# Dividing the probabilities of late heads by their sums, and a second q and k set for odd early heads, in a planned fp32r attention and MLP kernel

## The chip, the cores and the metric

The kernel runs on one core of a Trainium2 chip. The metric is device time in microseconds (us), the median of three runs. Engines are called as in the profile: PE (TensorE matmuls), PEld (its weight loads), DVE (VectorE), ACT (ScalarE), POOL (GpSimd), SP (the queue that issues all DMAs).

## What is computed

Three stages follow one another on 4 batches of 8 heads, 576 positions and 64 values a head, all in fp32:

```python
scores = q @ k.T / 8 + (cum[i] - cum[j])    # cum: running sum of log(clip(f)); causal mask
attn = exp(scores - max); attn /= sum(attn) + 1e-9
x = attn @ v                                # heads side by side: 2304 tokens x 512
x = ((x @ w1) * (x @ w2)) @ w3 @ w_out      # 512 -> 1024 -> 1024 -> 512
x = x / rms(x) * g
out = (silu(x @ w_gate) * (x @ w_val)) @ moe2_w_out   # 512 -> 1536 -> 512
```

## The kernel before

**Number format.** Every fp32 operand of a matmul is split into a high and a low part of the type fp32r, and a product takes two or three matmuls. So each matrix that TensorE reads costs two more passes of another engine: a copy that gives the high part, and a difference that gives the low part.

**A head.** `prep` makes Q1 (high part of q/8 on partitions 0 to 63, low part on 64 to 127), Q2, K1 and K2 from the loaded q and k: Q1's high part (line 348) and K1 (line 349) on ACT, Q2 (line 238, through `scaled`) and K2 (line 230, through `sub`) on an engine that the planner picks, Q1's low part on DVE (line 352). Four more rows of Q2 and K2 carry cum, so that the matmuls of `attn_s` (lines 367 and 368) give scores with their decay. There is one set of Q1, Q2, K1, K2 for all heads: `prep` of a head can't write it before the matmuls of the head before have read it. `row_max` (DVE, line 384) adds the mask and takes the row maximum, `row_exp` (ACT, line 391) takes exp and the row sums. `attn_t` transposes the probabilities on PE (line 428) and splits them into PTh (ACT, line 431) and PTl (DVE, line 432). `pv` multiplies by v (lines 451 and 457) and adds two halves into x.

**The pair.** Two heads share a 128-row block of x. Once a pair is through, the inverse sums (lines 413 and 414) are spread by a copy into rcol (640 columns, through `scaled`), five matmuls transpose rcol (line 473, `normalize`), and DVE multiplies x by it from PSUM (line 477).

**The weights.** Twenty raw units of 1 MB (w3, w_out, then w1 with w2) are loaded as bit patterns and rebuilt by `unit`: ACT (line 496), DVE (lines 497 and 498), then the high part on ACT (line 504) and the low part by `sub`. `wc_group` forms w3 @ w_out on PE (line 557), evicted by lines 560 and 561. The first MLP is `ab_group` (line 590) and `y_group` (line 613), the second one line 714 and line 745.

**The order.** All operations go into a `Plan`. `begins` walks back from the end and gives each operation a latest begin; for PE operations the due time `at` can make it earlier. `order` simulates the engines with assumed durations and emits a static program order for each engine. An operation with several engines is only taken by one on which, in the simulation, it ends first:

```python
end = min(begin(i, x, k) + m for x, m, k in ops[i][0])
if t + ns > end + 1:
    continue
```

For such a copy of n columns the assumed durations are 95 + 0.833 n ns on ACT, 70 + 0.52 n on DVE, 170 + 0.83 n on POOL. Operations marked `lock` on DVE and all on POOL exclude each other in the simulation. Among those ready, an engine takes the one with the smallest latest begin plus `WAIT` times its wait. The due times come from constants: heads of the first batch every `TE`, later ones every `T1`, the groups of w3 @ w_out every `WCP` from `WC0`. The first MLP of batch 0 is due `FD` after the last head of batch 0, and heads of batch 1 are mixed with it.

Of the kernel before, what the change touches and what calls it, by code (L numbers as in the profile page):

```python
# [69 lines left out]
class Plan:  # L70
# [54 lines left out]
    def order(self):  # L125
# [10 lines left out]
        dma = 0  # L136
# [59 lines left out]
def body(ctx, tc, q, k, v, f, w12, w3, wo1, wgv, wo2, g, out):  # L196
# [9 lines left out]
    def pe(cols, fn, r=(), w=(), at=0, times=1):  # L206

        plan.op([("PE", times * (max(110, 0.4475 * cols) + 2), False)], lambda e: fn(), r, w, at)
# [81 lines left out]
    Wch = [m1.tile([P, DM], F32R, name=f"Wch{i}") for i in range(KF)]  # L290
    Wcl = [m1.tile([P, DM], F32R, name=f"Wcl{i}") for i in range(KF)]
# [38 lines left out]
    def make_qk_rows():  # L330
        for t in (Q2, K2):
            V.memset(f32(t)[D:P, :], 0.0)
# [12 lines left out]
    def prep(h, at):  # L345
        p = h % 2
        a, b_ = rq[p][0:D], rk[p]
        act(S, lambda: A.activation(Q1[0:D, :], a, AF.Copy, scale=0.125), [("rq", p)], ["Q1h"], at)
        act(S, lambda: A.copy(K1, b_), [("rk", p, 0), ("rk", p, 1)], ["K1"], at)
        scaled(S, Q2[0:D, :], a, 0.125, [("rq", p)], ["Q2"])  # L350
        low = dict(out=Q1[D:P, :], in0=a, scalar=0.125, in1=f32(Q1[0:D, :]), op0=ALU.mult, op1=ALU.subtract)
        dve(S + 100, lambda: V.scalar_tensor_tensor(**low), [("rq", p), "Q1h"], ["Q1l"], at, lock=True)
        sub(S, K2[0:D, :], b_[0:D], f32(K1[0:D, :]), [("rk", p, 0), "K1"], ["K2"])
        if h:
            dma(9200, lambda: SP.dma_start(out=f32(Q2[D:D + 4, :]), in_=cq_d[h]), ["cdq"], ["rowq"], at)
            dma(9200, lambda: SP.dma_start(out=f32(K2[D:D + 4, :]), in_=cn_d[h]), ["cdn"], ["rown"], at)

    QK = ["Q1h", "Q1l", "Q2", "K1", "K2", "rows", "rowq", "rown"]

    def prep_v(h, at):  # L360
        p = h % 2
        scaled(5 * D, V2[p][:, :, 0:D], rv[p], 1.0, [("rv", p)], [("V2h", p)])
        sub(5 * D, V2[p][:, :, D:P], rv[p], f32(V2[p][:, :, 0:D]), [("rv", p), ("V2h", p)], [("V2", p)])

    def s_main(o, i, k0, k1):
        q0, n = QB[i]
        T.matmul(o, Q1[:, q0:q0 + n], K1[:, k0:k1], start=True, stop=False)  # L367
        T.matmul(o, Q2[:, q0:q0 + n], K2[:, k0:k1], start=False, stop=True)  # L368

# [7 lines left out]
    def row_max(h, ap, i, key, at):  # L377
# [4 lines left out]
        if len(ap.shape) == 3:  # L382
            o, m = (x.rearrange("p (c n) -> p c n", c=2) for x in (o, m))
        dve(cols + 12, lambda: V.tensor_tensor_reduce(out=o, in0=ap, in1=m, scale=-1.0, scalar=-NEG, op0=ALU.add, op1=ALU.min, accum_out=nmax[p][:n, i:i + 1]),  # L384
            ["mask"], [("nmax", p, i), ("PB", p, i), key], at)

    def row_exp(h, i, at):
# [3 lines left out]
        act(cols + 110, lambda: A.activation(o, o, AF.Exp, bias=nmax[p][:n, i:i + 1], scale=-1.0, accum_out=rsum[pr][:n, p, i:i + 1]),  # L391
            [("nmax", p, i)], [("PB", p, i), ("rsum", pr, p, i)], at)

    def attn_s(h, at):
        p = h % 2
        t = wide.rearrange("p (c n) -> p c n", c=2)
# [45 lines left out]
    def pv(h, at):  # L442
        p, j, (b, pp) = h % 2, h % 2, divmod(h // 2, H // 2)
        t = wide
# [14 lines left out]
        pe(192, tail, [(a, c) for a in ("PTh", "PTl") for c in (PT_KB0, PT_KB3)] + [("V2", p), ("V2h", p)], ["wide"], at, 2)  # L459
        x_to, x_key = X[b % 2][j * D:(j + 1) * D, pp, :], ["wide", ("x", b % 2, pp, j)] + [("raw", "x1")] * (b == 1)  # L460
        act(S, lambda: A.copy(half, t[D:P, 0:S]), [], ["half", "wide"], at, 55)
        dve(S + 100, lambda: V.tensor_add(x_to, t[0:D, 0:S], half), ["half"], x_key, at)

    def normalize(h, at):
# [3 lines left out]
        t = wide  # L468
# [7 lines left out]
        pe(128, run, ["rcol"], ["wide"], at, 5)  # L476
        dve(S, lambda: V.tensor_mul(x, x, t[:, 0:S]), [], ["wide"] + [("x", b % 2, pp, j) for j in range(2)], at)
# [3 lines left out]
    def unit(raw, key, src, h_l, outkey, at, at_load, r_load=(), w_load=(), r_out=(), over=None, parts=1):  # L481
# [14 lines left out]
        act(1024, lambda: A.activation(f32(hi()), f32(hi()), AF.Prelu, scale=2.0**-112, alpha=2.0**32), [key], [kh], at)  # L496
# [3 lines left out]
        for c in range(parts):  # L500
# [48 lines left out]
    def wc_group(i, at, step):  # L549
# [10 lines left out]
        act(512, lambda: A.copy(Wch[i], o), [], [("bank", n), ("Wch", i)], at)  # L560
        dve(512, lambda: V.tensor_sub(Wcl[i], o, f32(Wch[i])), [("Wch", i)], [("bank", n), ("Wcl", i)], at)
# [3 lines left out]
    speed = [FR]  # L565
# [15 lines left out]
    def ab_group(b, c, fb, m):  # L581
# [23 lines left out]
    def y_group(b, c, eb):  # L605
# [160 lines left out]
    def attention(h):  # L766
        if h < NH:
            attn_s(h, s_at(h))
        if h:
# [3 lines left out]
            if h % 2 == 0:  # L773
# [8 lines left out]
    def start():  # L782
# [6 lines left out]
        dve(1150, make_qk_rows, w=["rows", "Q2", "K2"], at=-100)  # L789
# [4 lines left out]
        dve(300, lambda: V.tensor_copy(hi.bitcast(F32R), cum), ["cum"], ["cq0"], -100)  # L794
        dve(S, lambda: V.tensor_sub(lo.bitcast(F32R), cum, hi), ["cum", "cq0", "cq1"], ["cq"], -100)
# [25 lines left out]
    start()  # L821
    units = [("w3", 0)] + [("wo", i) for i in range(4)] + [("w3", i) for i in range(1, KF)] + [("w12", i) for i in range(KF)]
    where = ["nrm", "ul", "x", "x1"][:NRAW]
    for n, (kind, i) in enumerate(units):
# [3 lines left out]
        raw = where[n % NRAW] if n < 16 else "nrm" if i % 2 else "w3"  # L828
        {"w3": w3_unit, "wo": wo_unit, "w12": w12_unit}[kind](i, raw, 0, 0)
# [106 lines left out]
```

## Time and profile before

| | before |
|---|---|
| median of 3 runs | 1038.04 us (1037.55 to 1038.85) |
| profiled execution | 1038.35 us, its span 1036.6 us |
| PE busy | 992.6 us, 96% of the span |
| DVE busy | 555.5 us, 54% |
| ACT busy | 466.1 us, 45% |
| POOL busy | 186.8 us, 18% |

The time is that of the program with what lies around its span, here 1.75 us more than the span. A share of the whole span is a mean over stages: heads and weights come first, the second MLP fills the last 450 us.

### The profile page before, as it was taken

To read this page: it belongs to the slowest core of one execution; us is meant where nothing else is said; L and a number is where in the kernel's file an instruction comes from. 1 tells how busy PE (TensorE), PEld (TensorE's weight loads), DVE (VectorE), ACT (ScalarE), POOL (GpSimd) and SP (SyncE) were. 2 spreads that over 40 slices of the span, in tenths; PEclk is the share of its full clock that TensorE was granted. 3 is DMA by queue.
4 is the path that set the end of the run, shared out by engine and by line. 5 is a ranking of instruction groups with operands and counts; after the bars stand their busy time and mean duration, and the time that the engine had idled before them with its cause. 6 is when DMAs were issued, how large, how long until landed. Compare 5 with 4: busy or idle time off the path is not lost.

```text
span 1036.6 us, 15402 instructions
## 1 busy us (share of the span) xinstructions
PE 992.6 (96%) x5928; PEld 886.8 (86%) x5928; DVE 555.5 (54%) x1104; ACT 466.1 (45%) x1004; POOL 186.8 (18%) x222
## 2 busy tenths in 40 slices
PE   1799979999999999999999999999999999999997
PEld 1578869999999999999999888878888888888896
DVE  6889999757668676776557445532122112211121
ACT  4778887656665665665445434421121112111111
POOL 3535433322523132240220300000000000000000
PEclk9999989999999999999999999999999999999999
DMA  8554533111212121200432324312001000100000
GB/s 271 184 189 134 181 116 120 49 36 51 71 37 61 48 60 39 59 15 1 170 120 105 136 109 162 104 59 84 1 1 41 1 1 0 41 1 1 17 25 21
DMA packets 28161, 75.71 MB, mean 73 GB/s; under 512 B 3644, under 2 KB 12348, under 8 KB 23160
## 3 DMA queue, kind: packets, MB, share of 16 engines
q1 hardware_dynamic: 28088, 74.73, 22.1%
q8 instruction: 46, 0.75, 0.3%
q14 instruction: 27, 0.22, 0.1%
HBM read 64.69 MB, written 10.03 MB: 72 GB/s over the span
## 4 chain that ended last, share of the span: by engine, by line
PE 91%; DVE 6%; DMA 1%; ACT 1%; issue 1%; POOL 0%; ACTq 0%; DVEq 0%; POOLq 0%
PE bank L714 29%; PE bank L590 19%; PE bank L613 10%; PE wide L745 8%; PE bank L745 6%; PE bank L428 5%; PE wide L451 4%; PE bank L557 3%; PE bank L368 1%; PE bank L367 1%; PE wide L473 1%; PE wide L367 1%; PE wide L368 1%; PE wide L457 1%; DMA rk<-in_k 1%
## 5 line engine op out<-in xcount | busy, mean ns | idle before, releaser
L721 DVE TENSOR_TENSOR s<-bank,s 128x512 f32<-128x512 f32 (+1 forms) x60 | 38.3, 638 | 281.3 <-PE bank L714 281.3
L714 PE MATMUL bank<-xnh,wgh 128*128 128x512 f32 (+1 forms) x480 | 177.6, 370 | 0.0
L714 PE MATMUL bank<-xnl,wgh 128*128 128x512 f32 (+1 forms) x480 | 177.6, 370 | 0.0
L714 PE MATMUL bank<-xnh,wgl 128*128 128x512 f32 (+1 forms) x480 | 177.2, 369 | 0.0
L720 ACT ACTIVATE s<-bank 128x512 f32<-128x512 f32 (+1 forms) x60 | 33.3, 555 | 189.4 <-PE bank L714 189.2
L714 PEld LDWEIGHTS bank<-xnh,wgh 128*128 128x128 f32 x480 | 90.2, 188 | 16.9
L714 PEld LDWEIGHTS bank<-xnl,wgh 128*128 128x128 f32 x480 | 90.3, 188 | 16.4
L714 PEld LDWEIGHTS bank<-xnh,wgl 128*128 128x128 f32 x480 | 90.2, 188 | 16.1
L431 ACT CAST PTh<-bank 128x320 fp32r<-128x320 f32 (+3 forms) x128 | 64.7, 506 | 86.5 <-PE bank L428 74.4
L722 ACT CAST zh<-s 128x512 fp32r<-128x512 f32 (+1 forms) x60 | 34.7, 578 | 129.7 <-DVE s L721 129.7
L432 DVE TENSOR_TENSOR PTl<-bank,PTh 128x320 fp32r<-128x320 f32 (+3 forms) x128 | 74.7, 588 | 22.2 <-ACT PTh L431 21.4
L613 PE MATMUL bank<-uh,Wch 128*128 128x288 f32 x256 | 77.2, 302 | 0.0
L613 PE MATMUL bank<-ul,Wch 128*128 128x288 f32 x256 | 75.5, 295 | 0.0
L613 PE MATMUL bank<-uh,Wcl 128*128 128x288 f32 x256 | 75.3, 294 | 0.0
L723 DVE TENSOR_TENSOR zl<-s,zh 128x512 fp32r<-128x512 f32 (+1 forms) x60 | 39.1, 652 | 30.4 <-ACT zh L722 30.0
L451 PE MATMUL wide<-PTh,V 128*128 128x512 f32 (+4 forms) x160 | 53.2, 338 | 0.6 <-DVE nmaxb L384 0.5
L451 PE MATMUL wide<-PTl,V 128*128 128x512 f32 (+4 forms) x160 | 49.6, 326 | 1.9 <-DVE PTl L432 1.9
L596 ACT COPY a<-bank 128x288 f32<-128x288 f32 x64 | 25.6, 400 | 52.7 <-PE bank L590 52.4
L745 PE MATMUL wide<-wo2h,zh 128*128 128x512 f32 x120 | 47.9, 399 | 0.7 <-ACT o L755 0.7
L613 PEld LDWEIGHTS bank<-uh,Wch 128*128 128x128 f32 x256 | 48.1, 188 | 0.4
L613 PEld LDWEIGHTS bank<-ul,Wch 128*128 128x128 f32 x256 | 48.2, 188 | 0.3
L598 DVE TENSOR_TENSOR u<-bank,a 128x288 f32<-128x288 f32 x64 | 29.1, 455 | 35.5 <-PE bank L590 30.5
(281 smaller groups left out, 2589.2 us busy)
## 6 DMA issues: line engine op xcount, KB each, us to landing
raw<-in_wgv SPq DMA_DIRECT2D x12, 1024.0 KB
rk<-in_k SPq DMA_DIRECT2D x64, 144.0 KB
raw<-in_wo SPq DMA_DIRECT2D x6, 1024.0 KB
nrm<-in_w SPq DMA_DIRECT2D x5, 1024.0 KB
rv<-in_v SPq DMA_DIRECT2D x32, 160.0 KB
rq<-in_q SPq DMA_DIRECT2D x32, 144.0 KB
yn_d<-nrm SPq DMA_DIRECT2D x8, 576.0 KB
raw<-yn_d SPq DMA_DIRECT2D x4, 1024.0 KB
```

The source lines that it names most:

```text
L428: T.transpose(o[:, c * P:(c + 1) * P], PB[p][i][:, kb * P:(kb + 1) * P], ident)
L431: act(n, lambda: A.copy(PTh[:, pt:pt + n], o[:, lo:lo + n]), [], [("PTh", pt), key], at, 55)
L432: dve(n, lambda: V.tensor_sub(PTl[:, pt:pt + n], o[:, lo:lo + n], f32(PTh[:, pt:pt + n])), [("PTh", pt)], [("PTl", pt), key], at)
L451: pe(w, lambda s_=s_, o=o, w=w, c=c, kb=kb, m=m, src=src: T.matmul(t[:, o:o + w], V2[p][:, kb, :], src[:, c:c + w], start=(s_ == 0 and m = ...
L590: T.matmul(o, a, x[:, kt, :], start=(kt == 0 and i == 0), stop=(kt == KD - 1 and i == 2))
L613: T.matmul(o, a[:, es], x[:, ft, :], start=(ft == 0 and i == 0), stop=(ft == KF - 1 and i == 2))
L714: T.matmul(t[m], a[:, m, kt, :], x[:, kt, 0:n], start=(kt == 0 and i == 0), stop=(kt == KD - 1 and i == 2))
L720: act(n, lambda: A.activation(s_()[:, 0:n], t[0], AF.Silu), [("bank", b_[0]), "right"], ["s"], at)
L721: dve(n, lambda: V.tensor_mul(s_()[:, 0:n], t[1], s_()[:, 0:n]), [("bank", b_[1])], ["s"], at)
L722: act(n, lambda: A.copy(zh()[:, 0:n], s_()[:, 0:n]), ["s"], [("zh", zp)], at)
L723: dve(n, lambda: V.tensor_sub(zl()[:, 0:n], s_()[:, 0:n], f32(zh()[:, 0:n])), ["s", ("zh", zp)], [("zl", zp)], at, lock=True)
L745: T.matmul(acc2[t], a[:, ts_], w, start=(fb == 0 and i == 0), stop=(fb == KF2 - 1 and i == 2))
```

## The change

For heads from 8 on (`LATE`), the sums are inverted head by head, and the five probability blocks of the head (64, 192, 320, 448 and 576 columns) are multiplied by them in place, by copies with a free engine, before they are transposed. These pairs have no rcol, no transposes of it and no product on x. Heads 0 to 7 keep the old way.

In batch 0, odd heads get a q and k set of their own (`qk2`, in space that the first MLP uses later as `uh`). Its zero rows are set by DVE or POOL. The factor 1/8 leaves `prep` and goes into `row_max`; cum is scaled by 8 to fit. Q1's high part, K1 and the high parts of rebuilt weights become copies with a free engine, and Q1's low part a difference on DVE or POOL. At the start, the high part of cum goes to ACT, and the negated rows to a free engine.

The planner's constants change, several assumed durations become longer (the scores of 512 columns to 680 and 570, exp by 115 columns), and a rule is added: before it takes an operation that begins later, an engine takes one that fits ahead of it, with `SLIP` of overrun. After `MT` the simulated hand-over between engines is longer by 600 and 300 ns and not by 321 and 133.

```diff
+LATE = 8
-S0, TE, T1 = 14000, 11400, 14300
-LT, LP = 8000, 10500
-WC0, WCP = 30000, 9400
-FD, FR = 14000, 1.48
-WAIT = 2.0
-COLD = 19378
-MT, MARGIN, MARGIN2 = 135119, 321, 133
+S0, TE, T1 = 0, 9000, 14300
+LT, LP = 5000, 13000
+WC0, WCP = 20000, 9400
+FD, FR = 14000, 1.35
+WAIT, SLIP = 2.0, 800
+DMA0, COLD = 4500, 26000
+MT, MARGIN, MARGIN2 = 135000, 600, 300
...
+                fits = [c for c in can if c[0] < t and c[0] + c[2] < t + SLIP]
+                if fits:
+                    t, i, ns, lock = min(fits, key=lambda c: (by[c[1]] + WAIT * (c[0] - first), c[1]))
...
+    qk2 = get("qk2", m1, [P, 4, S], F32R, tag="uh", name="qk2")
+    def qk_of(h):
+        i = h % 2 if h < H else 0
...
-        act(S, lambda: A.activation(Q1[0:D, :], a, AF.Copy, scale=0.125), [("rq", p)], ["Q1h"], at)
-        act(S, lambda: A.copy(K1, b_), [("rk", p, 0), ("rk", p, 1)], ["K1"], at)
-        dve(S + 100, lambda: V.scalar_tensor_tensor(**low), [("rq", p), "Q1h"], ["Q1l"], at, lock=True)
+        copy(S, lambda: Q1()[0:D, :], a, [("rq", p), ("rows", s_)], [("Q1h", s_)])
+        copy(S, K1, b_, [("rk", p, 0), ("rk", p, 1), ("rows", s_)], [("K1", s_)])
+        sub(S, lambda: Q1()[D:P, :], a, lambda: f32(Q1()[0:D, :]), [("rq", p), ("Q1h", s_)], [("Q1l", s_)])
...
+        if h >= LATE:
+            sums, inv = rsum[pr][:, p], rinv[pr][:, p]
+            dve(10, lambda: V.tensor_scalar_add(inv, sums, 1.0e-9), ...)
+            dve(80, lambda: V.reciprocal(inv, inv), [], [("rinv", pr, p)], at)
+            for i in (1, 2, 3, 4, 0):
+                n, cols = QB[i][1], QEND[i]
+                o = PB[p][i][:n, 0:cols]
+                copy(cols, o, o, [("rinv", pr, p)], [("PB", p, i)], rinv[pr][:n, p, i:i + 1])
...
-            act(n, lambda cs=cs: A.copy(h_l()[0][:, cs], f32(lo()[:, cs])), [key, kl] + r_out, wh, at)
+            copy(n, lambda cs=cs: h_l()[0][:, cs], lambda cs=cs: f32(lo()[:, cs]), [key, kl] + r_out, wh)
...
-            if h % 2 == 0:
+            if h % 2 == 0 and h <= LATE:
                 normalize(h - 1, at + LP)
...
-        dve(300, lambda: V.tensor_copy(hi.bitcast(F32R), cum), ["cum"], ["cq0"], -100)
+        act(S, lambda: A.activation(hi.bitcast(F32R), cum, AF.Copy, scale=8.0), ["cum"], ["cq0"], -100)
-        dve(S, lambda: V.tensor_scalar_mul(cn[:, 1::2, :], cq[:, 0::2, :], -1.0), ["cq", "cn1"], ["cn"], -90)
+        copy(2 * S, cn[:, 1::2, :], cq[:, 0::2, :], ["cq", "cn1"], ["cn"], -1.0)
```

## Rows read from the trace of the kernel before

**Rows 1.** The profile page: span and busy time of each engine.
```profile
span 1036.6 us, 15402 instructions
...
PE 992.6 (96%) x5928; PEld 886.8 (86%) x5928; DVE 555.5 (54%) x1104; ACT 466.1 (45%) x1004; POOL 186.8 (18%) x222
```

**Rows 2.** Stretches: length, then PE, PEld, DVE, ACT, POOL busy, clock, DMA.
```profile
15.00:60.00 45.00, 30.17 (x134) 24.02 (x135) 38.83 (x72) 33.37 (x67) 16.78 (x16) 0.92 0.69 225
60.00:130.00 70.00, 69.08 (x399) 58.65 (x398) 62.25 (x133) 58.03 (x140) 32.35 (x37) 1.00 0.48 157
130.00:155.00 25.00, 18.02 (x109) 15.52 (x110) 24.45 (x47) 20.12 (x38) 7.58 (x7) 0.86 0.35 117
155.00:200.00 45.00, 44.28 (x331) 42.73 (x330) 38.69 (x76) 31.42 (x72) 16.05 (x15) 1.00 0.29 89
200.00:500.00 300.00, 300.00 (x2276) 294.26 (x2275) 207.08 (x501) 177.74 (x458) 82.71 (x99) 1.00 0.17 48
```

**Rows 3.** Timeline of PE: start, us, what; idle before and its releaser.
```profile
14.92 0.58 PE L367 MATMUL wide<-K,Q 128*128 128x288 f32 x1 [14.92 <-DVE Q L352]
...
16.49 0.58 PE L368 MATMUL wide<-K,Q 128*128 128x288 f32 x1 [0.99 <-DVE K L810]
...
143.16 0.82 PE L590 MATMUL bank<-xhl,W0h 128*128 128x288 f32 x2 [4.35 <-DVE Wcl L561]
```

**Rows 4.** Line 473, transposes of rcol: ns min/median/max, first and last start.
```profile
L473 PE MATMUL wide<-ident,rcol x80: 270/272/328, 53.7 to 491.7; 128*128 128x128 f32 x80
```

**Rows 5.** Timeline of PE around the last such group: start, us, what.
```profile
491.24 0.71 PE L473 MATMUL wide<-ident,rcol 128*128 128x128 f32 x5
491.70 0.38 PE L613 MATMUL bank<-uh,Wch 128*128 128x288 f32 x1
491.92 0.29 PE L613 MATMUL bank<-ul,Wch 128*128 128x288 f32 x1
492.05 0.29 PE L613 MATMUL bank<-uh,Wcl 128*128 128x288 f32 x1
```

**Rows 6.** DVE's groups up to 150 us: busy us, mean ns, idle before.
```profile
L352 DVE SCALAR_TENSOR_TENSOR Q<-rq,Q 64x576 fp32r<-64x576 f32 x11 | 8.5, 772 | 1.5 <-ACT Q L348 1.1
...
L498 DVE SCALAR_TENSOR_TENSOR x<-x 128x1024 uint32<-128x1024 uint32 x4 | 6.2, 1560 | 0.0
...
L498 DVE SCALAR_TENSOR_TENSOR raw_x<-raw_x 128x1024 uint32<-128x1024 uint32 x4 | 4.9, 1222 | 0.1
...
L497 DVE TENSOR_SCALAR raw_x<-raw_x 128x1024 uint32<-128x1024 uint32 x4 | 4.1, 1029 | 0.0
...
L497 DVE TENSOR_SCALAR nrm<-nrm 128x1024 uint32<-128x1024 uint32 x4 | 2.7, 687 | 0.0
...
L794 DVE CAST x<-tmp 68x576 fp32r<-68x576 f32 x1 | 1.6, 1608 | 0.0
...
L813 DVE TENSOR_SCALAR x<-x 32x1152 f32<-32x1152 f32 x1 | 0.7, 747 | 0.0
```

**Rows 7.** The longest wait of DVE from 15 to 150 us.
```profile
DVE PTl L432 <- ACT PTh L431: 6.0, 15, 0.8
```

**Rows 8.** Line 238, copies of which the planner picks the engine: ns min/median/max.
```profile
L238 POOL TENSOR_SCALAR Q<-rq x32: 663/667/677, 7.3 to 454.2; 64x576 fp32r<-64x576 f32 x32
L238 POOL TENSOR_SCALAR V<-rv x27: 447/458/1397, 13.2 to 460.6; 128x320 fp32r<-128x320 f32 x27
L238 DVE TENSOR_SCALAR rcol<-rinvb x6: 819/820/821, 78.1 to 476.6; 128x640 f32<-128x640 f32 x6
L238 DVE TENSOR_SCALAR rcol<-rinva x4: 820/820/822, 52.7 to 451.4; 128x640 f32<-128x640 f32 x4
```

**Rows 9.** Line 230, the differences K2 that went to POOL.
```profile
L230 POOL TENSOR_TENSOR K<-rk,K x22: 1388/1422/2454, 9.5 to 459.2; 64x576 fp32r<-64x576 f32 x22
```

**Rows 10.** ACT's copies of q and k up to 150 us.
```profile
L348 ACT ACTIVATE Q<-rq 64x576 fp32r<-64x576 f32 x11 | 7.5, 684 | 1.3 <-issue 1.2
L349 ACT CAST K<-rk 128x576 fp32r<-128x576 f32 x11 | 7.4, 671 | 0.1
```

More of the change, by code (lines that the diff above doesn't have):

```diff
@@ L206, in pe @@
     def pe(cols, fn, r=(), w=(), at=0, times=1):
[L208 removed]
+        plan.op([("PE", times * (max(110, 0.4475 * cols) + 2), False)], lambda e, times=times: fn(), r, w, at)
     def t_dve(n, rate=1.04, lock=False):
@@ L328, in make_zeros, with get, fn, make_qk_rows @@
             G.memset(t, 1.0)
-    def make_qk_rows():
+    lazy = {}
+    def get(key, pool_, shape, dtype, **kw):
+        def fn():
+            if key not in lazy:
+                lazy[key] = pool_().tile(shape, dtype, **kw) if callable(pool_) else pool_.tile(shape, dtype, **kw)
+            return lazy[key]
+        return fn
+    Wch = get("Wch", m1, [P, KF, DM], F32R, name="Wch")
+    Wcl = get("Wcl", m1, [P, KF, DM], F32R, name="Wcl")
+    qk2 = get("qk2", m1, [P, 4, S], F32R, tag="uh", name="qk2")
+    def qk_of(h):
+        i = h % 2 if h < H else 0
+        t = (lambda: qk1, qk2)[i]
+        return *(lambda t=t, m=m: t()[:, m] for m in range(4)), i
+    def make_qk_rows(h, on=V):
+        _, Q2, _, K2, _ = qk_of(h)
         for t in (Q2, K2):
-            V.memset(f32(t)[D:P, :], 0.0)
+            on.memset(f32(t())[D:P, :], 0.0)
     def load_qk(h, at):
@@ L361, in prep_v, with s_main @@
         p = h % 2
-        scaled(5 * D, V2[p][:, :, 0:D], rv[p], 1.0, [("rv", p)], [("V2h", p)])
+        copy(5 * D, V2[p][:, :, 0:D], rv[p], [("rv", p)], [("V2h", p)])
         sub(5 * D, V2[p][:, :, D:P], rv[p], f32(V2[p][:, :, 0:D]), [("rv", p), ("V2h", p)], [("V2", p)])
-    def s_main(o, i, k0, k1):
+    def s_main(h, o, i, k0, k1):
         q0, n = QB[i]
-        T.matmul(o, Q1[:, q0:q0 + n], K1[:, k0:k1], start=True, stop=False)
-        T.matmul(o, Q2[:, q0:q0 + n], K2[:, k0:k1], start=False, stop=True)
+        Q1, Q2, K1, K2, _ = qk_of(h)
+        T.matmul(o, Q1()[:, q0:q0 + n], K1()[:, k0:k1], start=True, stop=False)
+        T.matmul(o, Q2()[:, q0:q0 + n], K2()[:, k0:k1], start=False, stop=True)
     ring = [0]
@@ L395, in attn_s @@
         p = h % 2
-        t = wide.rearrange("p (c n) -> p c n", c=2)
+        t, wk = wide, ["wide"]
+        t = t.rearrange("p (c n) -> p c n", c=2)
+        QKh = [(x, qk_of(h)[4]) for x in QK]
         n1, n2 = st_next(), st_next()
@@ L457, in tail @@
                 T.matmul(t[:, 512:704], V2[p][:, 0, :], src[:, PT_Q0:PT_Q0 + 192], start=(m == 0), stop=(m == 1))
-        pe(192, tail, [(a, c) for a in ("PTh", "PTl") for c in (PT_KB0, PT_KB3)] + [("V2", p), ("V2h", p)], ["wide"], at, 2)
-        x_to, x_key = X[b % 2][j * D:(j + 1) * D, pp, :], ["wide", ("x", b % 2, pp, j)] + [("raw", "x1")] * (b == 1)
-        act(S, lambda: A.copy(half, t[D:P, 0:S]), [], ["half", "wide"], at, 55)
+        pe(192, tail, [(a, c) for a in ("PTh", "PTl") for c in (PT_KB0, PT_KB3)] + [("V2", p), ("V2h", p)], wk, at, 2)
+        x_to, x_key = X[b % 2][j * D:(j + 1) * D, pp, :], wk + [("x", b % 2, pp, j)] + [("raw", "x1")] * (b == 1)
+        act(S, lambda: A.copy(half, t[D:P, 0:S]), [], ["half"] + wk, at, 180)
         dve(S + 100, lambda: V.tensor_add(x_to, t[0:D, 0:S], half), ["half"], x_key, at)
@@ L475, in normalize @@
         x = X[b % 2][:, pp, :]
-        pe(128, run, ["rcol"], ["wide"], at, 5)
-        dve(S, lambda: V.tensor_mul(x, x, t[:, 0:S]), [], ["wide"] + [("x", b % 2, pp, j) for j in range(2)], at)
+        pe(128, run, ["rcol"], wk, at, 5)
+        dve(S, lambda: V.tensor_mul(x, x, t[:, 0:S]), [], wk + [("x", b % 2, pp, j) for j in range(2)], at)
     def unit(raw, key, src, h_l, outkey, at, at_load, r_load=(), w_load=(), r_out=(), over=None, parts=1):
@@ L821, in body, with weights @@
     start()
+    def weights(units):
+        for kind, i, raw in units:
+            {"w3": w3_unit, "wo": wo_unit, "w12": w12_unit}[kind](i, raw, 0, 0)
     units = [("w3", 0)] + [("wo", i) for i in range(4)] + [("w3", i) for i in range(1, KF)] + [("w12", i) for i in range(KF)]
-    where = ["nrm", "ul", "x", "x1"][:NRAW]
+    where = ["nrm", "ul", "x", "x1"]
     for n, (kind, i) in enumerate(units):
@@ L827, in body @@
                 attention(h)
-        raw = where[n % NRAW] if n < 16 else "nrm" if i % 2 else "w3"
-        {"w3": w3_unit, "wo": wo_unit, "w12": w12_unit}[kind](i, raw, 0, 0)
+        weights([(kind, i, where[n % 4] if n < 16 else "nrm" if i % 2 else "w3")])
         if (kind, i) == ("wo", 3):
```

93 lines of the change are left out of this document (42 added, 51 removed).

## The prediction, made before the result was known

> **What bounds the kernel now.** I read the page first. PE is busy 992.6 of 1036.6 us [rows 1], so what can be won is either PE work or the 44 us in which PE does nothing. The stretches place these: the first matmul begins at 14.9 us [rows 3]; then PE is idle 45.0 - 30.2 = 14.8 us up to 60, 0.9 up to 130, 7.0 up to 155, 0.7 up to 200, and not at all from 200 to 500 [rows 2]. Together 38.3 us, all ahead of 200.
>
> So there are two regimes. From 155 us PE sets the time: each microsecond of PE work that goes is a microsecond of the end, and work on other engines is free as long as PE finds its operands. Ahead of 155 it is DVE: from 15 to 155 us it is busy 38.8 + 62.3 + 24.5 = 125.5 of 140 us, 90%, where ACT has 111.5 (80%) and POOL 56.7 (40%) [rows 2]. The wait that shows it is that of the first MLP, which begins at 143.2 us after 4.35 us of waiting for DVE [rows 3]; until then PE has eaten what heads and w3 @ w_out gave it. If DVE gets through this stage earlier by some time, the first MLP starts earlier by as much, and PE loses that much less.
>
> The profiled execution (span 1036.6, time 1038.35 us) lies 0.3 us above the median of 1038.04; I add all terms to the median. About 0.2%, 2.1 us, is what can be told from no change.
>
> **Part 1: the transposes that go.** There were 16 pairs with five transposes, 80 in all, the last at 491.7 us [rows 4]. Pairs of heads 0 to 7 stay; 12 groups go. One group takes PE from 491.24 to 491.70, and the matmul behind it takes 0.22 until the next where 0.13 is usual [rows 5]: 0.46 + 0.09 = 0.55 us. The twelve belong to batches 1 to 3, and by the due times they run mixed with the first MLP, where PE is full [rows 2]. 12 x 0.55 = 6.6 us, rounded to **-6.5 us**. If some of them sat in idle PE time, it would be less; the bound below is 5.5 (10 groups).
>
> **Part 2: the divisions that come.** Each of 24 heads gets five copies, 1600 columns. By the copies of q (576 columns in 0.667 us on POOL [rows 8], 0.684 on ACT [rows 10]) that is 1.85 to 1.9 us; on DVE, by line 497 (1024 columns in 0.687 [rows 6]), about 1.1. So 26 to 46 us of work, of which a part replaces 12 spreads of rcol (0.82 us on DVE [rows 8]) and 12 products on x. From 200 to 500 us, DVE is busy 207, ACT 178, POOL 83 of 300 us [rows 2]: 430 us of idle time cover it. I cost it at nothing. Queued behind the copies on DVE are the PTl of other heads, and PE waits for these; but the planner orders PE with them in mind and has the MLP to run in between. Without this cover it would cost up to 26/24 = 1.1 us a head.
>
> **Part 3: the start.** In DVE's work ahead of the first MLP:
> - the cast of cum's high part leaves DVE: -1.6 us [rows 6]; the negated rows leave it: -0.75 [rows 6];
> - Q1's low part, 11 times, 8.5 us [rows 6], becomes a choice of DVE or POOL. Of the K2 differences, which had that choice, 22 of 32 went to POOL [rows 9]: -8.5 x 22/32 = -5.9;
> - the zero rows of the second set come, on DVE or POOL, 1152 columns as the negated rows have (0.75 [rows 6]): between 0 and +0.75, half of it, +0.4;
> - copies that were ACT's may now come to DVE: 22 of q and k (7.5 + 7.4 us on ACT [rows 10]) and the high parts of 16 units. All on DVE, at the rate of line 497, they are 22 x 0.39 + 16 x 0.69 = 19.6 us. Of the copies that were free before, all 32 of Q2 and 27 of 32 of V went to POOL, none of these to DVE; of rcol, 10 of 16 to DVE [rows 8]. That is 10 of 80, 1 in 8: +2.4;
> - POOL then has some 3/4 of the copies (33 us at 0.667 for 576 columns, so 25) and the 7.6 differences at 1.42 [rows 9], together 36 us more beside the 56.7 it has. What that does to DVE is bounded by the rows so: below, the stretch that is seen (line 497 takes 4.1 us for the four of raw_x and 2.7 for the four of nrm, line 498 6.2 for x and 4.9 for raw_x [rows 6], 2.7 us beside 56.7 us of POOL, so 1.7); above, 36, if each microsecond of POOL stops DVE for one. K2 on POOL itself goes from 1.39 to 2.45 us [rows 9], so there is more than I summed. I take +3, near the seen end.
>
> Sum: -1.6 - 0.75 - 5.9 + 0.4 + 2.4 + 3.0 = -2.4 us of DVE work, at 90% busy -2.6 us of time.
>
> DVE also waits for ACT: 6.0 us in 15 waits of PTl for PTh [rows 7]. ACT loses copies, an engine now fills a gap with what fits, and odd heads' `prep` needn't wait for the matmuls of the head before. That gives back between nothing and 6; I take 3. The first head itself starts earlier too: its second matmul waits for DVE until 16.49 [rows 3], and without cast, negation and Q1's low part ahead of it this is about 2.4 us earlier; that is the same DVE time, not counted twice. Start: -2.6 - 3.0, **-5.5 us**.
>
> **Part 4: constants.** Due times of heads, of w3 @ w_out and of the MLP all move forward, by about 10 to 33 us. Only their order among each other does anything. The last two of the eight groups of w3 @ w_out now fall due behind the MLP's begin; each takes 5.5 us of PE work (24 matmuls of 512 columns, by the 0.13 us of 288 columns [rows 5]) and some 3.4 us of DVE work (0.69 + 1.22 [rows 6], and 1.5 for low parts and eviction at the rate of line 498) out of the stage ahead of it, which costs PE 5.5 - 3.4/0.9 = 1.7 us. Against that stand fewer stalls by longer assumed durations. I set both to zero, bounds +3.4 and -3. The longer hand-over after `MT` moves PE's operands earlier than needed; PE is full there, so nothing. The DMA queue SP has the same transfers; odd heads' two row loads come earlier.
>
> Total: 1038.0 - 6.5 - 5.5 = **1026 us**.
>
> **The rivals.**
> A: *The start gives nothing.* POOL's new work takes from DVE what it relieves it of. It happens once the stretch is 8 us and not 3, that is 0.22 us for each microsecond of POOL. For it: line 498 at 1.56 against 1.22 us [rows 6]. Against: the planner knows an exclusion of the two engines and gives POOL only what ends first there. Then only the transposes are left: 1038.0 - 6.5 = 1031.5, with +-3 for part 4.
> The Trainium skill speaks for this rival: SBUF — State Buffer, section "Who interferes with whom", says that DVE and GpSimd share one port pair, that a DVE instruction with two SBUF inputs or in a two-port mode and a GpSimd instruction exclude each other, and that the one that comes second blocks fully. By that rule the stretch would lie towards the upper bound, and the time nearer to 1032 than to 1026; the sum above goes by the seen stretch.
>
> B: *Slower: the copies land on DVE.* By the planner's durations a copy ends first on DVE whenever DVE is free (70 + 0.52 n is the lowest line). If all 19.6 us go there, DVE's balance is -2.4 + 17.2 = +14.8, so +16.4 us; with -6.5 and -3 the end is at about 1045. It decides from 13 of the 19.6 us on, two copies in three. For it: rcol, 10 of 16 on DVE. Against: the 64 others, none [rows 8], and that DVE is the engine that is least often free.
>
> C: *Much faster.* DVE does without the cost on POOL and the copies, and all its waits on ACT go: (-8.3 - 6.0)/0.9 = -16 us, 1038 - 6.5 - 16 = 1015, down to 1010.
>
> **How the numbers follow.** Forecast (1026, itself 1018 to 1030) 0.45; A 0.20; C 0.14; B 0.16; and 0.05 that the two parts cancel, B at about two thirds, within 0.2%. So faster 0.79, same 0.05, slower 0.16. The range goes from C's lower end to the edge of "same", 1010 to 1037, and leaves out B and a little of C.
>
> **What the profile of the changed kernel would show.** Part 1: the line of the transposes of rcol x20 and not x80, PE's busy sum lower by 6 to 7 us in its full stretch. Part 2: PE without idle time from 200 to 500 us; if it has some behind PTl or PTh, the cover was missing. Part 3: the first MLP's begin at about 137 and not 143 us, PE's idle time ahead of 200 us at about 33, Q1's low part mostly on POOL, POOL near 65% from 15 to 155 us. A: PE's idle time unchanged, lines 497 and 498 longer. B: copies of q, k and weights on DVE in two of three cases, DVE full and the first MLP later. The prediction is wrong in its ground if DVE is not what the first MLP waits for.

## The result, and the profile after

The changed kernel takes 1022.0 us (1021.4 to 1024.3, median of 4 runs) against 1038.4 us before, again the median of 4 runs: ratio 0.9846, 95% interval 0.9829 to 0.9863, 16 us less. The forecast was 1026 in 1010 to 1037. The profiled execution has a span of 1019.6 us. The page of it: busy time, then 40 slices of PE and of its granted clock.

```profile
span 1019.6 us, 15375 instructions
...
PE 981.6 (96%) x5868; PEld 877.7 (86%) x5868; DVE 589.8 (58%) x1251; ACT 457.7 (45%) x1007; POOL 151.0 (15%) x195
...
PE   1789999999999999999999999999999999999997
...
PEclk9999999999999999999999999999999999999999
```

PE's busy time fell from 992.6 to 981.6 us [rows 1], its idle time from 44.0 to 38.0: 11.0 and 6.0 make the 17.0 us between the spans. The transposes of rcol are 20, as forecast (line 506 is line 473 of before):

```profile
L506 PE MATMUL wide<-ident,rcol x20: 270/273/328, 49.5 to 120.0; 128*128 128x128 f32 x20
```

Sixty fewer at 0.55 us for five are 6.6 of the 11.0 us. The other 4.4, what is left by this estimate, are not work that went: the granted clock was higher. The stretches tell where (after the engines PE, PEld, DVE, ACT, POOL comes the granted clock):

```profile
15.00:60.00 45.00, 31.09 (x164) 25.25 (x165) 43.73 (x95) 34.18 (x75) 19.03 (x19) 1.00 0.71 231
60.00:130.00 70.00, 68.81 (x400) 58.00 (x399) 67.88 (x157) 56.51 (x130) 30.84 (x40) 1.00 0.46 145
130.00:155.00 25.00, 23.73 (x164) 21.96 (x164) 24.81 (x45) 20.64 (x43) 6.72 (x6) 1.00 0.53 190
155.00:200.00 45.00, 43.20 (x314) 40.65 (x313) 38.27 (x87) 28.99 (x74) 13.11 (x16) 1.00 0.23 67
200.00:500.00 300.00, 300.00 (x2265) 295.53 (x2264) 227.13 (x592) 188.55 (x480) 59.86 (x73) 1.00 0.17 51
```

Against [rows 2], the clock from 15 to 60 us is 1.00 and not 0.92, and from 130 to 155 it is 1.00 and not 0.86. Before, PE had gone idle for 2.7 us ahead of 53.7 us and for 4.35 ahead of 143.2 [rows 3], and ran the next stretches at a lower grant:

```profile
53.65 0.74 PE L473 MATMUL wide<-ident,rcol 128*128 128x128 f32 x5 [2.69 <-ACT PB1a L391]
```

```profile
55.00:60.00 5.00, 5.00 (x20) 4.03 (x19) 4.87 (x7) 2.99 (x7) 2.15 (x3) 0.66 0.68 245
...
140.00:145.00 5.00, 1.84 (x8) 1.87 (x9) 5.00 (x6) 3.94 (x11) 1.71 (x2) 0.54 0.70 239
```

The sum of the prediction had no term for this. PE's idle time from 130 to 155 us fell from 7.0 to 1.3, and from 155 to 200 it rose from 0.7 to 1.8. From 200 to 500 us there is none, as foreseen.

Then DVE. Its work ahead of the first MLP's first matmul, at 143.16 us before and at 131.5 after, and from 15 to 155 us; first before:

```profile
0.00:143.16 143.16, 106.07 (x575) 88.23 (x576) 122.83 (x242) 107.11 (x229) 64.19 (x86) 0.97 0.59 188
15.00:155.00 140.00, 117.27 (x640) 98.19 (x641) 125.54 (x251) 111.52 (x243) 56.71 (x58) 0.95 0.53 172
```

and after:

```profile
0.00:131.50 131.50, 102.00 (x569) 84.77 (x570) 122.56 (x269) 99.80 (x214) 58.16 (x87) 1.00 0.60 190
15.00:155.00 140.00, 123.62 (x724) 105.20 (x725) 136.42 (x295) 111.33 (x246) 56.59 (x64) 1.00 0.55 180
```

This is the main reading: 122.8 us of DVE work before, 122.6 after, done in 143.2 and in 131.5 us. DVE was not relieved of anything on balance; it stood still 20.3 us before and 8.9 after. From 15 to 155 us it is 97% busy and not 90%. In the changed kernel the first MLP begins at 131.5 us without waiting for DVE. Of DVE's waits, PTl for PTh was 6.0 us [rows 7] and is 0.4:

```profile
DVE w L243 <- PE bank L581: 0.6, 2, 0.3
DVE PTl L465 <- ACT PTh L464: 0.4, 1, 0.4
```

Where the free copies and differences went, up to 155 us: Q1's low part and K2 (line 234), and the copies of q and k on POOL and DVE (line 243) and on ACT (line 241).

```profile
L234 DVE TENSOR_TENSOR qk<-rq,qk x10: 751/752/1554, 7.3 to 153.5; 64x576 fp32r<-64x576 f32 x10
L234 DVE TENSOR_TENSOR qk<-rk,qk x10: 737/746/1194, 8.8 to 154.3; 64x576 fp32r<-64x576 f32 x10
...
L234 POOL TENSOR_TENSOR qk<-rk,qk x2: 1418/1464/1510, 35.9 to 69.0; 64x576 fp32r<-64x576 f32 x2
L234 POOL TENSOR_TENSOR qk<-rq,qk x2: 1420/1562/1703, 62.3 to 94.9; 64x576 fp32r<-64x576 f32 x2
```

```profile
L243 POOL TENSOR_SCALAR qk<-rq x6: 660/675/1162, 14.0 to 146.9; 64x576 fp32r<-64x576 f32 x6
...
L243 POOL TENSOR_SCALAR qk<-rk x6: 667/672/847, 44.2 to 146.2; 128x576 fp32r<-128x576 f32 x6
...
L243 DVE TENSOR_SCALAR qk<-rq x4: 453/744/1112, 6.8 to 34.9; 64x576 fp32r<-64x576 f32 x4
...
L243 DVE TENSOR_SCALAR qk<-rk x2: 437/448/459, 8.3 to 35.3; 128x576 fp32r<-128x576 f32 x2
```

```profile
L241 ACT ACTIVATE qk<-rq x14: 671/683/692, 6.8 to 146.1; 64x576 fp32r<-64x576 f32 x14
...
L241 ACT ACTIVATE qk<-rk x4: 665/674/690, 13.5 to 79.0; 128x576 fp32r<-128x576 f32 x4
```

Q1's low part is on DVE in 10 of 12 cases, where I expected 3 in 10. Of these 36 copies DVE has 6, 1 in 6, near the forecast 1 in 8. The high parts of the weights, which were free as well, are not in these lines; of them DVE has 11 pieces of 256 columns and two of 1024 ahead of the first MLP. Ten of them:

```profile
L243 DVE TENSOR_SCALAR w<-nrm x5: 285/286/294, 22.5 to 93.7; 128x256 fp32r<-128x256 f32 x5
L243 DVE TENSOR_SCALAR w<-raw_x x5: 275/286/1517, 69.0 to 114.0; 128x256 fp32r<-128x256 f32 x5
```

With the copies of q and k, those of Q2 among them, these are 9.9 us on DVE ahead of the first MLP, and not the forecast 2.4. POOL has 56.6 us of work from 15 to 155 us, as before (56.7); it didn't grow by 36.

### The profile page after: what moved, and what is told of

Read it like the earlier page. It is cut to its first block, busy times and chain, and to the rows that moved or that the text cites. A ratio compares the mean times of both kernels' runs of the same rounds, so it can differ in the third digit from the quotient of the medians.

```text
span 1019.6 us, 15375 instructions
## 1 busy us (share of the span) xinstructions
PE 981.6 (96%) x5868; PEld 877.7 (86%) x5868; DVE 589.8 (58%) x1251; ACT 457.7 (45%) x1007; POOL 151.0 (15%) x195
## 4 chain that ended last, share of the span: by engine, by line
PE 86%; DVE 11%; issue 1%; DMA 1%; SPq 1%; ACT 0%; DVEq 0%
PE bank L738 29%; PE bank L614 18%; PE bank L637 10%; PE wide L769 8%; PE bank L769 7%; PE bank L461 4%; PE wide L484 4%; PE bank L581 2%; DVE PTl L465 1%; PE bank L390 1%; PE bank L389 1%; DVE qk L234 1%; PE wide L389 1%; PE wide L390 1%; DVE x L495 1%
## 5 line engine op out<-in xcount | busy, mean ns | idle before, releaser
L746 ACT CAST zh<-s 128x512 fp32r<-128x512 f32 (+1 forms) x60 | 34.7, 578 | 131.7 <-DVE s L745 131.7
L465 DVE TENSOR_TENSOR PTl<-bank,PTh 128x512 fp32r<-128x512 f32 (+3 forms) x128 | 71.9, 584 | 23.0 <-ACT PTh L464 22.7
L464 ACT CAST PTh<-bank 128x512 fp32r<-128x512 f32 (+3 forms) x128 | 59.8, 505 | 26.1 <-PE bank L461 23.2
L484 PE MATMUL wide<-PTh,V 128*128 128x512 f32 (+4 forms) x160 | 49.6, 317 | 0.4 <-DVE nmaxb L406 0.2
L637 PEld LDWEIGHTS bank<-uh,Wcl 128*128 128x128 f32 x256 | 48.1, 188 | 0.0
L769 PE MATMUL wide<-wo2h,zl 128*128 128x512 f32 x120 | 47.5, 396 | 0.0
```

The costliest lines, as they stand in the source:

```text
L464: act(n, lambda: A.copy(PTh[:, pt:pt + n], o[:, lo:lo + n]), [], [("PTh", pt), key], at, 55)
L465: dve(n, lambda: V.tensor_sub(PTl[:, pt:pt + n], o[:, lo:lo + n], f32(PTh[:, pt:pt + n])), [("PTh", pt)], [("PTl", pt), key], at)
L637: T.matmul(o, a[:, es], x[:, ft, :], start=(ft == 0 and i == 0), stop=(ft == KF - 1 and i == 2))
L746: act(n, lambda: A.copy(zh()[:, 0:n], s_()[:, 0:n]), ["s"], [("zh", zp)], at)
L769: T.matmul(acc2[t], a[:, ts_], w, start=(fb == 0 and i == 0), stop=(fb == KF2 - 1 and i == 2))
```

## The experiments

The time is the median of a run, the ratio is against the kernel before on the same chip. The columns behind the ratio are read from the profiled execution, which in runs 2 and 12 was 2 us faster than the median. PE's idle time is span less busy time. The stretches are read as above.

| run | time, us | ratio (95%) | PE busy | PE idle | DVE busy 15 to 155 | first MLP at |
|---|---|---|---|---|---|---|
| before | 1038.4 | | 992.6 | 44.0 | 125.5 | 143.2 |
| changed kernel | 1022.0 | 0.9846 (0.9829 to 0.9863) | 981.6 | 38.0 | 136.4 | 131.5 |
| 1 changed, all pairs the old way | 1025.9 | 0.9879 (0.9864 to 0.9894) | 989.3 | 35.0 | 136.0 | 131.7 |
| 2 changed, no gap filling | 1039.3 | 1.001 (1.000 to 1.0019) | 987.0 | 48.6 | 126.7 | 141.1 |
| 3 changed, one q and k set | 1022.3 | 0.9842 (0.9825 to 0.9858) | | | | |
| 4 changed, copies pinned | 1019.7 | 0.9822 (0.9808 to 0.9837) | 979.8 | 38.1 | 136.1 | 132.7 |
| 5 changed, old due times | 1024.3 | 0.9867 (0.9852 to 0.9882) | 981.1 | 41.3 | 136.4 | 135.4 |
| 6 changed, old durations | 1022.9 | 0.985 (0.9833 to 0.9866) | 983.6 | 38.5 | 135.2 | 134.9 |
| 7 before, gap filling alone | 1020.3 | 0.9826 (0.9811 to 0.9841) | 987.1 | 30.9 | 136.4 | 129.3 |
| 8 before, late division alone | 1035.2 | 0.9972 (0.9961 to 0.9983) | 986.6 | 46.8 | 125.8 | 143.6 |
| 9 changed, constants moved a little | 1021.4 | 0.9837 (0.9822 to 0.9852) | 982.2 | 39.1 | 136.3 | 133.2 |
| 10 before, filling, division from head 8 | 1019.6 | 0.9819 (0.9803 to 0.9835) | 986.3 | 31.0 | 135.9 | 134.2 |
| 11 before, filling, division from head 16 | 1015.9 | 0.9782 (0.9767 to 0.9796) | 982.6 | 30.6 | 136.5 | 128.9 |
| 12 before, filling without overrun | 1036.5 | 0.9976 (0.9966 to 0.9987) | 992.9 | 39.5 | 129.1 | 137.2 |

The profiled execution of run 3 took 5.5 ms, so its trace is not read; its three others took 1021.5 to 1022.6 us.

**Run 1, the transposes in the new order.**

```diff
-LATE = 8
+LATE = NH
```

> The changed kernel, but all pairs keep the old way (spread, five transposes, product on x); everything else of the change stays. If the 60 transposes are a term of their own of 6.5 us, beside a start that gave the rest, this is 1028.5 us, PE's busy sum is 6.6 us higher than in the changed kernel and its idle time the same. If the divisions cost something that the predicted nothing hides, or their absence lets heads 8 and 9 through earlier, it is nearer to 1022. If the old way also hurts the start, it is above 1032.

Measured 1025.9, so the old way costs 3.9 us and not 6.5. PE's busy sum is 7.7 us higher, but its idle time is 3.0 lower: 1.6 of this from 155 to 200 us, where the divisions of batch 1 run in the changed kernel, and the rest from 15 to 60, where none runs and only the order differs. The term of the transposes is there; what comes with the divisions takes back 2.7 of its 6.6 us.

**Run 2, the rule taken away.**

```diff
-                if fits:
+                if False and fits:
```

> The changed kernel without the rule that fills a gap with an operation that fits ahead. The traces say that DVE did the same work ahead of the first MLP in both kernels (122.9 and 122.6 us) and lost 20.3 us to idle time before and 8.9 after. Theory fill: this rule is what closed the gaps; without it DVE is back at about 90% from 15 to 155 us, the first MLP begins near 140 us, and the time is 1029 to 1033. Theory choice: free choice of engine closed them; then this stays within 2 us of 1022.

Measured 1039.3, outside the 1029 to 1033 of the theory: not only the start's gain goes, all of it goes. Everything else in the change, transposes included, is together worth nothing measurable without this rule: PE's busy time falls by 5.6 us and its idle time rises by 4.6, of which 3.6 lie from 200 to 500 us, behind PTl. DVE is back where it was:

```profile
0.00:141.10 141.10, 107.53 (x575) 88.10 (x576) 122.18 (x248) 98.45 (x214) 77.70 (x109) 0.96 0.57 180
15.00:155.00 140.00, 117.69 (x647) 97.18 (x648) 126.74 (x260) 101.87 (x225) 66.00 (x78) 0.96 0.52 171
```

It did 122.2 us of work ahead of the first MLP, the same once more, and needed 141.1 us for it. POOL has 66 us from 15 to 155: without the rule more of the free work goes there, as the prediction thought, and it doesn't help.

**Run 3, one set of q and k.** `qk_of` returns set 0 for all heads, and the second set's zero rows are gone.

> The changed kernel with one set of Q1, Q2, K1, K2 for all heads. If the second set lets the preparation of odd heads run ahead and so fills gaps, the first MLP begins 3 to 6 us later and the time is 1025 to 1028. If what matters is fill or choice alone, it stays within 2 us of 1022, and loses nothing but the zero rows that are gone (1 us or less gained).

Measured 1022.3: the second set is worth nothing that can be told.

**Run 4, copies pinned.**

```diff
-        copy(S, lambda: Q1()[0:D, :], a, ...)
-        copy(S, K1, b_, ...)
-        sub(S, lambda: Q1()[D:P, :], a, ...)
+        act(S, lambda: A.activation(Q1()[0:D, :], a, AF.Copy), ...)
+        act(S, lambda: A.copy(K1(), b_), ...)
+        dve(S, lambda: V.tensor_sub(Q1()[D:P, :], a, f32(Q1()[0:D, :])), ..., lock=True)
...
-            copy(n, lambda cs=cs: h_l()[0][:, cs], ...)
+            act(n, lambda cs=cs: A.copy(h_l()[0][:, cs], f32(lo()[:, cs])), ...)
```

> The changed kernel with the engines of before: Q1's high part, K1 and the weights' high parts on ACT, Q1's low part on DVE. My prediction said that free choice relieves DVE; the trace shows DVE's share of these copies at about one in three and Q1's low part on DVE in 10 of 12, so no relief. Theory choice: copies go where an engine is idle and shorten chains; pinned, the time is 1026 to 1030. Theory fill: with the gaps filled, pinned copies cost nothing, and DVE has some 7 us less to do ahead of the first MLP; the time stays within 2 us of 1022 or falls below it.

Measured 1019.7, 2.3 us below the changed kernel, its interval just overlapping. Free choice of engine is not what gains; it gains nothing and may cost a little. This was the theory of the prediction's part 3. DVE's work ahead of the first MLP is 122.9 us again and not 7 us less, while POOL's is 44.4 us and not 58.2: the planner gives DVE other free work in place of the pinned.

**Runs 5 and 6, due times and durations.** Run 5 takes back `S0`, `TE`, `LT`, `LP`, `WC0`, `FR`; run 6 the assumed durations, `COLD`, `DMA0`, `MT`, `MARGIN`, `MARGIN2`.

> The changed kernel with the due times of before (heads, w3 @ w_out, first MLP). The prediction set their effect to zero, bounds +3.4 and -3. If that holds, this is 1019 to 1025. If the earlier due times are what moved the first MLP from 143 to 131 us, it begins near 140 again and the time is 1029 or more.

> The changed kernel with the assumed durations of before (scores, exp, reciprocals, ACT's fixed parts), the old hand-over after MT, the old end of the half clock and no first delay of the DMA queue. If a schedule that is nearer to the chip's durations is what removes PE's and DVE's stalls, this loses 4 to 8 us (1026 to 1030). If the order is as good with the old durations, it stays within 2 us of 1022.

Measured 1024.3 and 1022.9. The due times are worth 2.2 us at most, the intervals overlap, and that is within the bounds given; the durations are worth nothing that can be told.

**Run 7, the rule alone.**

```diff
+                fits = [c for c in can if c[0] < t and c[0] + c[2] < t + SLIP]
+                if fits:
+                    t, i, ns, lock = min(fits, key=lambda c: (by[c[1]] + WAIT * (c[0] - first), c[1]))
```

> The kernel before with the rule that fills gaps as its only change. Theory fill: the first MLP begins some 5 to 8 us earlier, DVE at 95% or more from 15 to 155 us, time 1029 to 1033. If the rule needs free engines or longer durations to work with, the time is 1036 to 1040.

Measured 1020.3 against 1038.0 on its chip: 17.7 us, beyond the 1029 to 1033 of the theory, with all 80 transposes, one set of q and k, and the old durations. The first MLP begins 13.9 us earlier.

```profile
0.00:129.30 129.30, 105.09 (x575) 85.95 (x576) 121.05 (x259) 107.61 (x234) 49.05 (x69) 1.00 0.64 210
15.00:155.00 140.00, 128.84 (x755) 109.13 (x756) 136.38 (x293) 122.19 (x273) 51.06 (x50) 1.00 0.58 190
155.00:200.00 45.00, 45.00 (x345) 44.27 (x344) 34.48 (x79) 31.35 (x79) 10.37 (x12) 1.00 0.15 43
```

Both accounts move: PE's idle time by 13.1 us, its busy time by 5.5 at a clock that now stays at 1.00. The rule holds for every engine's order, and ACT's work from 15 to 155 us rises too, from 111.5 to 122.2 us; that DVE's order alone carries the gain was not tested.

**Run 8, the division alone.**

```diff
-        if p:
+        if h >= LATE:    # five copies of the head's probabilities by 1 / sum
+        elif p:
...
-            if h % 2 == 0:
+            if h % 2 == 0 and h <= LATE:
```

> The kernel before with the division of late heads' probabilities as its only change. By the prediction's part 1, 60 transposes less are 6.5 us: 1031.5 to 1032, PE's busy sum 6.6 us lower, its idle time ahead of 200 us as before (38 us). If the divisions on DVE, ACT and POOL hold up the start, where heads 8 and 9 run, it is 1034 to 1038.

Measured 1035.2 against 1038.0: 2.7 us, under half of 6.5. PE's busy time fell by 6.0 us, its idle time rose by 2.8, 2.4 of it behind 130 us:

```profile
130.00:155.00 25.00, 16.63 (x92) 14.52 (x91) 24.80 (x42) 17.33 (x32) 7.02 (x7) 0.73 0.35 116
155.00:200.00 45.00, 43.23 (x319) 41.47 (x319) 42.04 (x91) 36.54 (x83) 10.25 (x13) 1.00 0.29 89
```

From 155 to 200 us DVE has 42.0 us of work and not 38.7 [rows 2], PE is idle 1.8 and not 0.7; from 130 to 155 us it is idle 8.4 and not 7.0, at a clock of 0.73. The divisions of batch 1, heads 8 to 15, fall where DVE is still full.

**Run 9, the order alone.** `MARGIN`, `MARGIN2`, `DMA0`, `COLD` at 580, 310, 4600, 25800.

> The changed kernel with four of the planner's constants moved by a little (hand-over 580 and 310 ns for 600 and 300, first DMA delay 4600 for 4500, end of the half clock 25800 for 26000). Nothing of the work changes. This measures how far a different order alone moves the time: if within 1 us of 1022, differences of 2 us between the other experiments are effects of what was edited; if it moves by 2 to 4 us, such differences say nothing.

Measured 1021.4. So 0.6 us is what one other order made; that is one sample, and I read nothing into differences of about 2 us or less.

**Runs 10 and 11, the rule with the division from head 8 and from head 16.** Run 7 with the edit of run 8, `LATE` at 8 and at 16.

> The kernel before with two changes: the rule that fills gaps, and late heads' probabilities divided from head 8 on. The rule alone gave 1020.3; the divisions alone gave 3.0 of the 6.5 us, since PE's idle time ahead of 200 us grew by 2.7. If the two add, 1017. If the divisions cost more where DVE has no gaps left (98% from 15 to 155 us with the rule), 1019 or more. If the rule hides them, 1014.

> As the run before, but probabilities are divided from head 16 on, so that batch 1, whose heads run while DVE is still full, keeps the old way: 40 transposes less, 4.4 us of PE work. Theory that the divisions cost time only where DVE is full: PE's idle time stays at that of the rule alone (25.6 us ahead of 200), time 1016. If they cost the same per head anywhere, half of the 2.7 us or more comes back, 1018.

Measured 1019.6 and 1015.9, against 1020.3 of run 7. From head 8 the division gives 0.7 us of its 6.6; from head 16 it gives 4.4 for 40 transposes, the full price. The first MLP begins at 134.2 us in run 10 and at 128.9 in run 11 (129.3 in run 7). Run 10, then run 11, from 130 to 200 us:

```profile
130.00:155.00 25.00, 21.82 (x147) 20.90 (x148) 24.59 (x44) 19.76 (x39) 7.05 (x8) 0.93 0.21 64
155.00:200.00 45.00, 44.95 (x340) 43.92 (x339) 36.31 (x88) 33.27 (x80) 13.57 (x15) 1.00 0.24 79
```

```profile
130.00:155.00 25.00, 24.44 (x183) 23.80 (x184) 24.06 (x51) 19.72 (x44) 8.59 (x8) 1.00 0.44 136
155.00:200.00 45.00, 45.00 (x345) 44.26 (x345) 34.22 (x79) 31.32 (x80) 9.91 (x12) 1.00 0.16 45
```

In run 10 PE is idle 3.2 us from 130 to 155 us and its clock is 0.93; in run 11 0.6 and 1.00. PE's idle time up to 200 us is that of run 7 all the same (25.6 us in both), since run 10 has 1.9 us less of it from 15 to 60 us, ahead of any division. What is lost shows in the busy time: 986.3 us with 20 transposes, 982.6 with 40. Not all of this is the divisions' doing: from 15 to 60 us, too, the clock of run 10 is lower than that of run 11, 0.96 and not 1.00. Run 11 is faster than both kernels, 6 us below the changed one.

**Run 12, filling without overrun.** Run 7 with `SLIP` at 0.

> The kernel before with the rule that fills gaps, but only with operations that end before the waiting one begins (no overrun of 800 ns). Most of DVE's operations take 0.2 to 1.3 us and its gaps are mostly under 1 us, so if the overrun is what lets the rule find something, half or more of the gain goes: 1028 to 1034. If ending in time is enough, within 2 us of 1020.3.

Measured 1036.5, beyond the 1028 to 1034 that was expected: 15 of the 17.7 us hang on the overrun. Operations that end inside a gap close some of them (DVE at 129.1 us of work from 15 to 155 us for 125.5); those that may make the planned next one up to 0.8 us late close nearly all (136.4).

## Why the prediction was right, point by point

**What bounds.** Right in the main: PE from about 155 us on, DVE ahead of it. In the kernels with a trace DVE's work ahead of the first MLP is 121 to 126 us, and the first MLP's begin goes with DVE's idle time. That PE loses as much less as the first MLP begins earlier holds only in part: it begins 11.7 us earlier, and PE's idle time ahead of 200 us falls from 38.4 to 32.6.

**Part 1.** Right in PE's work: 6.0 (run 8) to 7.7 us (run 1) of its busy time for the forecast 6.5, and 4.5 us for 40 of the 60 (run 11).

**Part 2.** Costed at nothing, and it took 2.7 us (6.6 less the 3.9 of run 1), 3.9 (6.6 less the 2.7 of run 8) or 5.9 (6.6 less the 0.7 of run 10), in runs 1 and 10 in part by another order ahead of any division. The cover was read from 200 to 500 us, but of the eight heads of batch 1, a third of all, most are divided ahead of that, from 116 us on, where DVE of the changed kernel is 97% busy up to 155 us and 85% up to 200; run 11, which leaves batch 1 out, pays nothing. The price of a copy was off as well. I took 0.39 us for 576 columns on DVE; the divisions measure:

```profile
L243 DVE TENSOR_SCALAR PB4b<-PB4b,rinvb x6: 506/516/521, 172.7 to 466.5; 128x576 f32<-128x576 f32 x6
...
L243 DVE TENSOR_SCALAR PB1a<-PB1a,rinvb x5: 304/306/315, 216.6 to 452.9; 128x192 f32<-128x192 f32 x5
...
L243 DVE TENSOR_SCALAR PB2a<-PB2a,rinvb x4: 372/372/378, 216.3 to 452.6; 128x320 f32<-128x320 f32 x4
...
L243 DVE TENSOR_SCALAR PB3a<-PB3a,rinva x4: 446/448/452, 247.6 to 420.3; 128x448 f32<-128x448 f32 x4
L243 DVE TENSOR_SCALAR PB0a<-PB0a,rinva x4: 239/242/243, 248.0 to 420.6; 64x64 f32<-64x64 f32 x4
```

0.52 + 0.45 + 0.37 + 0.31 + 0.24 = 1.9 us a head, not 1.1.

**Part 3.** PE's idle time came out near, 6.0 us less for the forecast 5.5, but not by its steps, so that is luck; 4.4 of clock come on top, for which there was no term. The step that failed is the sum of -2.4 us of DVE work: measured -0.3 (122.8 and 122.6), and hardly one of its terms held. Q1's low part stayed on DVE, 7.7 us before and 7.1 after, where -5.9 was taken. The copies brought 9.9 us and not 2.4. K2, which the sum left out, moved to DVE: 10 of 12 cases up to 155 us, where DVE had 4 up to 150. The stretch by POOL, taken as +3, left the lines from which it was read: ahead of the first MLP lines 497 and 498 took 0.81 and 1.38 us on the mean and now take 0.69 and 1.24 (lines 530 and 531), while others grew longer (line 835, below). And -2.4 at 90% is -2.7, not -2.6. K2 on DVE before, and line 531, whose group of x was at 1560 ns on the mean [rows 6]:

```profile
L230 DVE TENSOR_TENSOR K<-rk,K 64x576 fp32r<-64x576 f32 x4 | 3.0, 749 | 0.1
```

```profile
L531 DVE SCALAR_TENSOR_TENSOR x<-x x4: 1211/1216/1231, 45.8 to 138.3; 128x1024 uint32<-128x1024 uint32 x4
```

The step that carried the gain is the one that got half a sentence: DVE's waits and "an engine now fills a gap with what fits", taken as 3 us in 0 to 6. It is mis-sized by a factor of six: 17.7 us alone (run 7), and nothing is left without it (run 2). I bounded it by the one wait that the view names, 6.0 us; DVE's idle time from 15 to 155 us, 14.5 us, stood in the rows that I had quoted for its 90%. The first head wasn't earlier either:

```profile
8.77 0.61 PE L389 MATMUL wide<-qk 128*128 128x288 f32 x1 [8.77 <-DVE qk L243]
16.65 0.58 PE L390 MATMUL wide<-qk 128*128 128x288 f32 x1 [7.27 <-DVE qk L835]
```

Its first matmul starts at 8.8 us and not 14.9, its second at 16.65 and not 16.49, since, among others, the two last operations for it on DVE (line 835, which is line 810 of before) took 1.2 us each, and not 0.8, beside two copies of POOL. Their first one, and the copies:

```profile
14.17 1.20 DVE L835 SCALAR_TENSOR_TENSOR qk<-x,ident,qk 4x576 fp32r<-4x576 f32 x1
```

```profile
14.02 1.88 POOL L243 TENSOR_SCALAR qk<-rq 64x576 fp32r<-64x576 f32 x2
```

**Part 4.** Zero with +3.4 and -3; run 5 gives some 2 us to the new due times. Right within its bounds. But the two groups of w3 @ w_out hardly fell behind the first MLP: the last of their matmuls starts at 133.5 us, the first MLP at 131.5.

**The rivals.** A (the start gives nothing) didn't happen, and its cause was hardly tested: POOL's work didn't grow, and its sign, lines 497 and 498 longer, is absent. Where POOL's copies ran beside it, DVE did lengthen, 1.20 us for 0.81 in line 835, whose two inputs lie in SBUF. The Trainium skill says in SBUF — State Buffer, section "Who interferes with whom", that a DVE instruction with two SBUF inputs contends with a GpSimd instruction that reads SBUF; the trace agrees. B (copies land on DVE) happened by half: 9.9 of the 19.6 us, under the 13 from which it would decide. C's time, 1015, came out for run 11, by other means.

So the time was forecast 4 us too high, and that it is no more is luck, two errors of opposite sign: the order of the work was worth 15 us more than I gave it (17.7 for 3), and all else, to which I gave 9 us, nothing that can be told beside it (1022.0 with the rule, 1020.3 for the rule alone).

What stays open in part: why the rest of the change with the rule (1022.0) is no better than the rule alone (1020.3), although it has 60 transposes less. The traces place the loss. Up to 200 us PE is idle 32.6 us in the changed kernel and 25.6 in run 7; 1.8 of these 7.0 us lie from 155 to 200, among the divisions of batch 1, but 5.2 from 15 to 60 us, ahead of the first division. Run 7 in this stretch, then two of PE's waits in the changed kernel, nearly all of them in this stretch:

```profile
15.00:60.00 45.00, 36.27 (x176) 27.84 (x177) 43.51 (x91) 39.03 (x87) 16.87 (x17) 1.00 0.75 252
```

```profile
PE bank L461 <- DVE PTl L465: 4.4, 3, 3.4
...
PE bank L390 <- DMA qk<-cn_d: 2.5, 1, 2.5
```

Run 7 has 1.5 us of the first and none of the second, the load of the second head's rows of cum, which is issued at 29.0 us and in run 7 at 22.3. It is not the free choice of engine for the copies of q, k and weights, and not the due times: with either taken back, PE is idle 14.1 and 14.9 us there (runs 4 and 5), as in the changed kernel, 13.9. Which of the other edits of the start brings it was not tested.

## What to carry to other kernels

Ask of a static order how long the bound engine stands still, not only how much it has to do: here nearly equal work took 143 or 129 us, and a rule of three lines in the planner was worth 17.7 us, where the best edit of the work (run 11) gave 4.4. Bound such a term by the whole idle time of that engine, not by the longest named wait. Before moving work to an engine "with time to spare", read its busy share in the stretch where the moved work will run, and cut the move where that share is full, as run 11 does.

## What the runs showed of the hardware

Idle time of PE was paid twice. In run 7 against before, 13.1 us of idle time went and 5.5 us of busy time with it, since the granted clock stayed at 1.00, which is 2.4 GHz, where it had been 0.54 to 0.86 in the stretches of 5 us (35 to 45, 55 to 60 and 140 to 150 us) at and behind gaps of 2.6 to 4.4 us. No single long gap is needed: in run 10 the clock is 0.95 from 40 to 45 us and 0.70 from 45 to 50, where PE was busy 3.7 and 4.9 of 5 us and its longest wait was 0.6 us.

At the program's begin the clock column reads 1.00 although the transposes of the kernel before start 0.21 us apart there (24.76, 24.97 and 25.18 us), and 0.11 from 31.3 us on; in the changed kernel they are 0.21 us apart up to 34.3 us and 0.11 from 35.4 on. As the same transposes are 0.21 us apart at 56.7 us too, where the column reads 0.66, the starts tell the level of the first matmuls, the column doesn't.
